# A fused attention and two gated layers: the written order of eight batches, its products and its loads, rearranged

## Chip, cores and metric

One core of a Trainium2 chip. The metric is the device time of one execution in microseconds, lower is better. In the trace PE is TensorE, PEld its weight loads, DVE is VectorE, ACT ScalarE, POOL GpSimd and SP SyncE, which issues the loads and stores.

## What is computed

Batch 8, 8 heads, 576 tokens, head size 64, so 512 columns in all.

```python
kv  = einsum('bhsd,bhde', k, v)          # per head, k^T v
o   = q @ kv;  x = o / rms(o) * g_norm
gate = sigmoid(causal_conv5(x))          # 5 taps on the tokens, per column
x   = (gate * (x @ w_val)) @ w_out
h   = gelu(x @ w_in);  u, v = halves(h)
v_s = w_sg @ layernorm(v) + b_sg         # mixes the 576 tokens
out = x + (u * v_s) @ w_out2
```

## The kernel before

Products are made from fp32r pairs: every operand is split into a high part and a low part, and a 512-column product is 12 matmuls: for each of four 128-row chunks high by high, low weight by high, high by low (`gemm3`). The weights come as 64-bit numbers and are split on the chip too. Tokens go in four tiles of 128 (0 to 3) and a rest of 64 (4); 4 batches share a block of rests (XR), whose own products follow the batches.

The first part (attention, convolution gate, `w_val`, `w_out`, for batches 0 to 7) is written out by hand as a list of steps in `ORDER` and `STEADY`, run one after the other under a manual schedule. Each engine executes its own steps in this order; semaphores hold a step until its inputs are there. Nothing but the list moves a step past another. Behind the list follow batch 7's last products (`val`, then `out`), the rests of batches 4 to 7 and the second layer, which the tile framework's own scheduler places; it can put such later instructions between the last steps of the list.

A step's name is a letter, a batch and a tile or column block:

- `o` product q by kv (PE, 128-column fp32), `q` its squares (ACT), `r` sums (DVE), `m` mean (POOL with a star, else ACT), `w` root (POOL), `s` scale (DVE, with a star ACT), `t` transpose (PE).
- `h`, `x` high part and full copy of the transposed tile (ACT), `l` its low part (DVE). A `t`'s PSUM bank is free when all three have read it. There are eight banks.
- `p`: tap, `pbmj` is batch b, block m, tap j (tap 0 on ACT, 1 to 4 on DVE); `S` sigmoid (ACT). `gX`, `gL`, `gr` (written `g0X`) put the rest columns of x and of the gate into the block XR.
- `v` product with `w_val` (PE), `z` times gate (DVE), `Z`, `u` high and low part (ACT; DVE, with a star POOL), `y` product with `w_out` (PE), `Y` copy (ACT; the last of a batch stores it). `/a-n` is a part of a product. Batch 8 stands for the rests of batches 0 to 3.
- `kv` product k by v (PE), `k` its copies (ACT, some DVE). `a`, `b`, `D`: the steps that split `w_val`, `w_out` and, for pieces a to s, `w_in` and `w_out2`; digits 0 to 4 and `t` are DVE, `a` and `h` ACT, `s` POOL. `c` does the convolution weights. `~3` asks for three filler products.
- `L`: loads on SP's queue: `LK`, `LV`, `Lq`, `La`, `Lb`, `LD`, `Lcw`, `Lg`. K and V have one buffer each. `LM` is no load but a memset on POOL: 64 rows of V's last chunk are zero padding. `W30` is 30 filler products.

`Attention.load_kv` (L342) issues the memset right behind the loads for batches 0 to 2; for later batches the list has `LM3` to `LM7`. `load` (L851) and `act_part` (L896) turn names into instructions. The list ends with taps, sigmoids and weight pieces; its last PE step is `y63`, and `moe.val(0)` (v70, behind the list) comes next on PE.

Of the kernel before, what the change touches and what calls it, by code (L numbers as in the profile page):

```python
# [38 lines left out]
ORDER = """
W30 La0 La1 LK0a LV0a LK0b LV0b LK0c LV0c Lq0a Lq0b Lg La2 La3 Lb0 Lcw a1a a0a a01 a00 a10 kv0a a02 a11 a12 kv0b a13  # L40
a14 a03 k03b k01b a0h k02b k03a k02a k00b k01a k00a a04 o01~3 q01 o03 r01 a20 q03 LK1 o02 a2a r03 a21 q02 o04 a3a m01*
w01 a30 m03* r02 o00 q04 a31 a0l a22 a32 a23 m02* q00 w02 a1h Lq1 a1l s01* a0c w03 a33 r00 ca s02 r04 b0a a2h s03 a24
b01 t01 a3h t02 m00* m04 c0 Lb1 h02 w00 w04 t03~1 c1 a2l s00 h03 h01 a34 x01 b00 t00 c2 s04 x02 kv1 x03 x00 b02 h00
l03 c3 a1c b03 c4 b04 c5 k1b k1a t04 x04 a3l l02 p020 LK2 b1a o11 l01 l00 q11 o12 a3c o14 p021 p000 b10 g0X p022 q12
r11 b0h p023 p001 o13 a2c r12 p002 m12 b11 p024 p030 m11* w11 o10 q14 q13 b12 b0l r13 q10 Lb3 r10 w12 Lb2 p031 v01 b0c
m13* S02 Lq2 p003 b13 p010 m10 w13 s11* w10 v03 s13* p032 s10* p011 t11 kv2 LK3 LM3 v00 p004 p012 p033 b1h v02 S00 k2a
p013 s12* b14 b20 p014 S01 b1s p034 z01 r14 z00 k2b h11 b2a S03 t13 Z01 b1+ Z00 g0L m14* t10 b21 t12 x13 x11 w14 b30
h10 s14 o22 o21~3 u00* l11 g0r z03 h13 Z03 z02 l10 l13 t14 h12 o24 l12 o23 b22 u01* o20 Lq3 LDa LDb q24 x10 q23 b3a
r23 Z02 q22 u03* x14 q20 q21 x12 b31 m23* w23 b23 b32 r22 b24 r21 r20 u02* m20* p110 b33 p120 r24 v11 p111 v12 p121
b2h p112 p122 p100 s23* m24 m21* y01 b2s p101 p123 b2+ p124 w21 p130 y00 s21* Y01 v13 p131 w20 m22* g1X b34 S12 y02  # L50
Y00 p132 w24 t23 b3h b3s s24* w22 t21 p113 p133 s22* b3+ p102 p134 y03 p114 Y02 s20* g1L S11 h23 p103 v10 h21 z11 p104
z12 l21 Z11 t22 S13 Z12 z13 S10 l23 Z13 h22 t24 z10 u11* t20 Z10 l22 u12* u10 h20 u13* x21 Y03 x23 x24 l20 x22 x20 g1r
"""

STEADY = """
kv3a/0-8 kv3a/8-12 kv3b y10 LK4 p220 y11 p210 p221 Daa p222 p230 k3 Da1 p211 p200 y12 p223 p212 Da0 Da2 p201 o30 p213
y13 Da3 q30 p202 p203 p224 r30 o31 p204 m30* v20 w30 p231 S20 q31 Da4 p214 Y12 r31 S21 o32 Dah z20 m31* Y13 Das v21
Z20 w31 p232 p233 s30 u20* o33 Dat LM4 s31 t30 q33 v22 Db0 h30 r33 q32 z21 m33* S22 w33 p234 Dba Y11 r32 g2X o34 Db1
S23 m32* s33 w32 Z21 t31 z22 v23 Y10 u21 g2r x31 g2L LDc Db2 q34 Lq4 Db3 Z22 x30 u22* kv4a/0-8 z23 Dbh h31 kv4a/8-12
s32 Z23 r34 kv4b Db4 m34* Dbs LDd t32 w34 u23 LK5 y20/0-11 h32 Dbt x32 Dca Dc1 Dc0 Dc2 t33 s34 y21/0-5 h33 l32 k4 l33  # L60
y20/11-1 y21/5-7 x33 Dc3 Dc4 Dch l31 LDe Dcs t34 y22 Dct x34 l30 p300 Dda p301 p310 p302 p320 o40 Y21 p303 y23 p330
p311 g3X Y20 Dd0 p312 q40 p304 o41 p321 S30 r40 v30 q41 p331 m40* w40 p322 Dd1 Dd2 p313 o42 r41 v31 q42 s40 m41* w41
Y22 z30 p323 p314 o43 p324 S31 Z30 t40 p332 v32 q43 r42 Y23 p333 S32 m42* u30* s41 r43 o44 z31 w42 z32 Z31 t41 Lq5 v33
p334 q44 m43* Z32 w43 Dd3 s42 Ddh S33 u31 g3r u32* s43 t42 r44 y30/0-9 Dds z33 m44* Dd4 Z33 LM5 Ddt LDf w44 h42 u33
t43 x42 y31/0-9 De0 Dea x40 s44 h41 g3L l42 x41 y30/9-2 x43 De1 y31/9-2 De2 y30/11-1 De3 y31/11-1 Deh t44 De4 y32 Des
LDg x44 Det p430 Df0 l41 p420 p410 y33 Dfa p411 p400 p431 Y32 Y31 p401 p412 v80 Y33 Df1 h40 Df2 p402 v81 p413 p421
kv5a/0-8 l40 kv5a/8-12 p403 kv5b p404 z80 v82 k5 z81 Y30 Df3 v83 Z81 z82 Z80 LK6 u81 Z82 u80* o50 z83 Dfh p414 o51 q50
Dfs h43 r50 y80/0-5 g4X u82* y81/0-5 l43 q51 y82/0-1 Z83 y80/5-1 r51 y81/5-1 y82/1-5 m50* Df4 w50 y83/0-4 Dft LDh
y80/6-2 p422 y81/6-2 Dga y82/6-2 y83/4-1 y80/8-1 Dg0 y81/8-1 m51* y82/8-1 u83 y83/5-2 w51 y80/9-2 y81/9-2 p432 y82/9-2
y83/7-4 Dg1 v40/0-3 Dg2 Dg3 Dgh y80/11-1 s50 y81/11-1 y82/11-1 y83/11-1 Dgs Y81 v40/3-9 S40 Dg4 s51 Y82 LDi Y83 p433  # L70
S41 o52 p423 t50 Dgt q52 t51 p424 Dha v41 Y80 p434 Dh0 Dh1 Dh2 Dh3 Dhh z40 Dhs o53 Z40 LM6 Dh4 v42 z41 LDj q53 r52 S43
Dht Z41 m52* g4L u40* Dia x51 h51 o54 Di1 w52 Di0 Di2 v43 r53 q54 Lq6 Dih Di3 S42 u41 Dis m53* Di4 w53 z42 LDk
kv6a/0-8 Dit Z42 kv6a/8-12 r54 Dja s52 h50 kv6b m54* u42* z43 x50 s53 t52 Z43 LK7 w54 Dj0 g4r Dj1 h52 Dj2 Dj3 Djh u43
y40 x52 LM7 Djs l50 s54 t53 Dj4 y41 x53 l52 LDl h53 Djt Dk0 Dka k6 Dk1 Dk2 Y40 Dk3 t54 l51 Dkh y42 x54 Dks l53 p500
Dk4 Dkt p520 LDm p501 p530 p502 o60 Dla Dl1 p531 y43 q60 p510 p532 p503 p521 o61 Dl0 r60 v50 p522 q61 m60* w60 g5X Dl2
p511 p504 p512 o62 p523 v51 q62 r61 S50 s60 m61* Y43 w61 p533 Y41 p524 o63 r62 t60 p513 q63 m62* v52 Dlh s61 S52 Dl3
Y42 p514 Dls z50 S51 r63 Z50 o64 Dl4 m63* w62 Dlt t61 Lq7 z51 v53 h61 LDn p534 Dma w63 q64 Dm0 g5L Z51 z52 x61 u51 S53
kv7a/0-8 u50* s62 h60 kv7a/8-12 z53 Z52 Dm1 kv7b r64 Z53 u52* l60 t62 s63 m64* y50/0-9 w64 x62 Dm2 u53 h62 Dm3 Dmh k7
Dms s64 t63 y51/0-4 Dm4 h63 Dmt LDo x60 y50/9-2 l63 Dna y51/4-2 Dn0 x63 y50/11-1 Dn1 y51/6-6 Dn2 g5r Dn3 Dnh l61 Dns
t64 l62 y52 x64 Dn4 Dnt LDp p600 p610 p601 Y51 p611 p630 o70 p602 Doa y53 p612 q70 Y50 Do0 p603 p620 Do1 p621 o71 p631  # L80
Do2 v60 q71 p613 Y52 r70 Doh p622 m70* w70 r71 o72 p614 v61 m71* Do3 S61 p604 w71 q72 s70 Y53 p623 S60 p632 o73 p624
t70 r72 q73 v62 S62 z60 m72* w72 h70 p633 Z60 s71 p634 o74 u60* r73 s72 t71 q74 v63 z61 Dos h71 z62 m73* g6r w73 Z61
r74 Z62 Do4 u61 S63 LDq m74* t72 x70 Dot y60/0-8 u62* s73 h72 z63 Dpa g6X w74 Dp1 Z63 l71 t73 Dp0 y61/0-8 u63 h73 Dp2
x73 s74 x71 Dp3 y60/8-1 l73 x72 y61/8-1 y60/9-2 Dph g6L y61/9-2 l72 Dps y60/11-1 y61/11-1 t74 Dp4 y62 Dpt LDr x74 Dq0
l70 p700 p710 p701 Dqa p711 Y61 y63 p730 Dq1 p712 Y62 p702 p720 Dq2 p721 Dqh Y63 Dq3 p722 Dqs Dq4 p713 Dqt p714 Dra
Y60 Dr0 p703 S71 LDs Dr1 p723 Dr2 p704 Drh Dr3 S70 p731 Drs p732 Dr4 p733 Drt p724 Dsa p734 S72 Ds1 S73 Ds0 Ds2
Ds3 Dsh Ds4 Dss Dst
"""
# [1029 lines left out]
```

## Time and profile before

| | us |
|---|---|
| median of 3 runs (716.17 to 716.47) | 716.29 |
| profiled execution | 717.12 |
| its span, first to last instruction | 715.3 |
| PE busy | 706.4 |
| DVE busy | 571.6 |
| ACT busy | 362.2 |
| POOL busy | 161.8 |
| mean DMA rate | 114 GB/s |

The written list takes the first 265 us of the span. An engine's idle time costs nothing unless it makes the engine wait that ends last, so the stretches have to be read one by one: which engine is full in each, and what the next product on PE waits for.

### The profile page before, as it was taken

Reading aid. Unit: us, or ns where it says so; the run is one execution under the profiler, and the core shown is the slowest. Engines: PE = TensorE matmul, PEld = TensorE weight load, DVE = VectorE, ACT = ScalarE, POOL = GpSimd, SP = SyncE. Lnnn points to the kernel's source line nnn. Section 1 sums busy time; section 2 is a strip of 40 time slices with the busy share of each in tenths; the row PEclk is TensorE's granted clock in tenths of the full one; section 3 lists DMA queues with packets and bytes.
Section 4 is the critical chain, followed back from the end, with each engine's and each line's share of the span. In section 5 each row is a group of like instructions: output and inputs, shape, how many; then the busy total and the mean of one; then the engine's idle time right before and its main releaser. Section 6 shows DMA issues by size and latency. Waiting matters only on the chain.

```text
span 715.3 us, 11743 instructions
## 1 busy us (share of the span) xinstructions
PE 706.4 (99%) x4462; PEld 618.3 (86%) x4462; DVE 571.6 (80%) x1111; ACT 362.2 (51%) x747; POOL 161.8 (23%) x180
## 2 busy tenths in 40 slices
...
GB/s 299 309 305 178 16 185 224 115 126 227 190 108 155 75 31 172 146 149 38 97 103 30 75 89 58 53 67 89 76 145 40 65 74 75 59 60 45 103 1 89
DMA packets 57241, 81.20 MB, mean 114 GB/s; under 512 B 3680, under 2 KB 30304, under 8 KB 56160
## 3 DMA queue, kind: packets, MB, share of 16 engines
...
HBM read 61.56 MB, written 18.87 MB: 112 GB/s over the span
## 4 chain that ended last, share of the span: by engine, by line
PE 90%; DMA 5%; DVE 3%; issue 1%; SPq 0%; ACT 0%; ACTq 0%
PE sg L740 17%; PE hv L631 14%; PE out L303 14%; PE y L303 12%; PE hu L303 12%; PE val L303 12%; PE o L400 4%; PE kv L379 2%; PE xT L436 2%; DMA Q<-in_qT_dram 2%; PE hur L303 2%; DMA V<-in_v_dram 1%; DVE G L499 1%; DMA raw<-in_w_in_dram 1%; DMA wiu<-in_w_val_dram 1%
## 5 line engine op out<-in xcount | busy, mean ns | idle before, releaser
L499 DVE SCALAR_TENSOR_TENSOR G<-X,cw,G 128x576 f32<-128x576 f32 x128 | 101.5, 824 | 4.2 <-ACT G L496 3.9
L303 PE MATMUL y<-Z,WOh 128*128 128x512 f32 (+1 forms) x320 | 96.5, 375 | 0.0
L643 POOL TENSOR_TENSOR bmv<-bmv,mhalf 128x1 f32<-128x1 f32 x36 | 20.1, 559 | 333.6 <-DVE bmv L642 333.6
L631 PE MATMUL hv<-wiv,X1h 128*128 128x512 f32 x256 | 83.1, 390 | 0.0
L303 PE MATMUL out<-Z,K 128*128 128x512 f32 x256 | 82.9, 389 | 0.0
L303 PE MATMUL hu<-X1h,wiu 128*128 128x512 f32 x256 | 79.4, 390 | 0.0
L421 POOL TENSOR_TENSOR st<-st,mhalf 128x8 f32<-128x8 f32 x40 | 73.0, 1838 | 2.2
L303 PEld LDWEIGHTS y<-Z,WOh 128*128 128x128 f32 x320 | 57.9, 188 | 9.8
L620 ACT ACTIVATE T<-T 128x512 f32<-128x512 f32 x68 | 43.0, 632 | 44.0 <-DVE T L617 43.8
L303 PE MATMUL y<-Z,WOl 128*128 128x512 f32 (+1 forms) x160 | 58.0, 368 | 0.0
L303 PEld LDWEIGHTS out<-Z,K 128*128 128x128 f32 x256 | 48.1, 188 | 9.9
L631 PEld LDWEIGHTS hv<-wiv,X1h 128*128 128x128 f32 x256 | 47.7, 188 | 9.8 <-ACT X1h L608 0.2
L303 PEld LDWEIGHTS hu<-X1h,wiu 128*128 128x128 f32 x256 | 46.6, 188 | 8.3
L741 DVE SCALAR_TENSOR_TENSOR T<-sg,gln,WOl 128x288 f32<-128x288 f32 x64 | 32.8, 516 | 24.8 <-PE sg L740 24.7
L303 PE MATMUL hu<-X1l,wiu 128*128 128x512 f32 x128 | 50.0, 390 | 0.0
L631 PE MATMUL hv<-wiv,X1l 128*128 128x512 f32 x128 | 49.9, 390 | 0.0
L303 PE MATMUL out<-Z,V 128*128 128x512 f32 x128 | 49.8, 389 | 0.0
L752 ACT ACTIVATE Z<-T 128x512 fp32r<-128x512 f32 x32 | 20.2, 631 | 58.2 <-DVE T L751 58.2
L400 PEld LDWEIGHTS o<-kvbd,Q 128*128 128x128 f32 x320 | 39.9, 191 | 2.6 <-ACT kvbd L391 0.5
L400 PE MATMUL o<-kvbd,Q 128*128 128x128 f32 x320 | 40.7, 275 | 0.3 <-ACT kvbd L391 0.3
L303 PE MATMUL val<-X0h,WV 128*128 128x512 f32 x128 | 40.7, 399 | 0.0
L303 PE MATMUL val<-X1h,WV 128*128 128x512 f32 x128 | 40.0, 396 | 0.1
...
## 6 DMA issues: line engine op xcount, KB each, us to landing
y_main<-Y SPq DMA_DIRECT2D x8, 1024.0 KB, 4.6
...
K<-in_k_dram SPq DMA_DIRECT2D x7, 1024.0 KB, 7.4
V<-in_v_dram SPq DMA_DIRECT2D x7, 1024.0 KB, 9.4
...
```

What stands on the lines that cost most here:

```text
L303: nc.tensor.matmul(ps, lhsT=a[:, kt, msl], rhs=x[:, kt], start=(i == 0), stop=(i == 3 * NK - 1))
L379: nc.tensor.matmul(self.pk[j][h, h], lhsT=self.k[:, t, js][:, h], rhs=self.v[:, t, js][:, h], start=(t == 0), stop=(t == 4))
L400: nc.tensor.matmul(po[:, j * P:(j + 1) * P], lhsT=self.q[:, j, o:o + P], rhs=bd[:, j, :], start=True, stop=True)
L421: nc.gpsimd.tensor_tensor(st[:, 2], st[:, 1], mhalf, op=ALU.pow)
L436: nc.tensor.transpose(pt[:, j * P:(j + 1) * P], i["xo"][:, j * P:(j + 1) * P], ident)
L499: stt(gate[:, m], x32[:, m, j:j + S], cw3[:, m, j:j + 1], gate[:, m], op0=ALU.mult, op1=ALU.add)
L620: act(w, w, AF.Tanh, scale=CG * AG)
L631: nc.tensor.matmul(ps, lhsT=a[:, kt], rhs=p2["wiv"][:, w, kt], start=(i == 0), stop=(i == 3 * NK - 1))
L643: nc.gpsimd.tensor_tensor(mv[:, 3:4], mv[:, 2:3], mhalf[:, 0:1], op=ALU.pow)
L740: nc.tensor.matmul(ps, lhsT=a[:, msl], rhs=w, start=(n == 0), stop=(n == len(mm) - 1))
L741: later(0, lambda: stt(vs[:, sl], ps, gln_s[:, m:m + 1], p2["bsg"][:, sl], op0=ALU.mult, op1=ALU.add))
L752: act(g[:, 0], x, AF.Copy)
```

## The change

`ORDER` and `STEADY` become one list with the same 1168 names in another order, and three new names, `LM0`, `LM1` and `LM2`: the memsets that `load_kv` did for batches 0 to 2 are now steps of their own. Every other step is there once, as before, with the same star and the same fillers. The o products of a batch now mostly stand together, the transposes too, and the tiles of a batch come in other sequences. Among the loads, V's first half leads, and `La1` follows batch 0's K and V. At the list's end `l71` and `l73` stand behind `y63`.

The diff, cut to the two lists' starts and ends and the code:

```diff
 ORDER = """
-W30 La0 La1 LK0a LV0a LK0b LV0b LK0c LV0c Lq0a Lq0b Lg La2 La3 Lb0 Lcw a1a a0a a01 a00 a10 kv0a a02 a11 a12 kv0b a13
-a14 a03 k03b k01b a0h k02b k03a k02a k00b k01a k00a a04 o01~3 q01 o03 r01 a20 q03 LK1 o02 a2a r03 a21 q02 o04 a3a m01*
-w01 a30 m03* r02 o00 q04 a31 a0l a22 a32 a23 m02* q00 w02 a1h Lq1 a1l s01* a0c w03 a33 r00 ca s02 r04 b0a a2h s03 a24
...
-"""
-
-STEADY = """
-kv3a/0-8 kv3a/8-12 kv3b y10 LK4 p220 y11 p210 p221 Daa p222 p230 k3 Da1 p211 p200 y12 p223 p212 Da0 Da2 p201 o30 p213
...
-r74 Z62 Do4 u61 S63 LDq m74* t72 x70 Dot y60/0-8 u62* s73 h72 z63 Dpa g6X w74 Dp1 Z63 l71 t73 Dp0 y61/0-8 u63 h73 Dp2
-x73 s74 x71 Dp3 y60/8-1 l73 x72 y61/8-1 y60/9-2 Dph g6L y61/9-2 l72 Dps y60/11-1 y61/11-1 t74 Dp4 y62 Dpt LDr x74 Dq0
-l70 p700 p710 p701 Dqa p711 Y61 y63 p730 Dq1 p712 Y62 p702 p720 Dq2 p721 Dqh Y63 Dq3 p722 Dqs Dq4 p713 Dqt p714 Dra
-Y60 Dr0 p703 S71 LDs Dr1 p723 Dr2 p704 Drh Dr3 S70 p731 Drs p732 Dr4 p733 Drt p724 Dsa p734 S72 Ds1 S73 Ds0 Ds2
-Ds3 Dsh Ds4 Dss Dst
+LV0a La0 LK0c LV0b Lcw W30 LK0a LV0c LK0b LM0 Lg La1 Lq0a a00 Lq0b La2 La3 Lb0 ca a0a c1 a01 a02 kv0a c0 a03 kv0b k03b
+k00a LK1 a1a k00b c2 k01b k03a k02a k02b k01a o01~3 a11 c3 a10 c4 a04 o00 a12 q01 a0h r01 o02 q00 a13 m01* a1h c5 r00
+w01 a0l q02 a2a o03 r02 m00* a14 o04 m02* q03 w02 a21 s01* r03 a1l Lq1 a20 Lb1 a22 m03* Lb2 w03 q04 s02 b0a r04 t02
+a2h t01 a23 LM1 a3a a30 w00 a24 h01 b01 h02 s03 m04 a1c a31 t03~1 w04 s00 x02 a2l a0c a32 x01 l02 t00 x03 s04 h03 b00
...
+s72 Z61 p634 u61 S63 t73 z62 t72 Dot v63 Z62 s74 x72 u62* s70 Dpa s71 x73 Dp0 g6r Dp1 h72 Dp2 t70 Dp3 Dph t74 Dp4 x70
+t71 Dps z63 LDr x74 y60/0-8 Dpt h70 l72 Dqa Z63 Dq0 Dq1 y61/0-8 x71 Dq2 u63 Dqh p730 Dq3 Dq4 Dqs p710 l70 LDs y60/8-1
+y61/8-1 Y53 y62 p731 p700 Dqt p732 Dra p701 Dr1 y61/9-2 Dr0 p702 y60/9-2 y61/11-1 Dr2 y60/11-1 p703 y63 Drh h71 Dr3
+p704 p720 Drs l71 Y62 Dr4 p711 Drt p721 Dsa Y60 Ds0 Ds1 Y63 p722 h73 Ds2 S70 p712 Dsh Y61 Ds3 p733 Dss l73 p713 p723
+p714 p734 S71 p724 S73 Ds4 S72 Dst
 """
...
@@ -863,7 +860,7 @@
             piece[0]()
             piece[2]()
         elif what in ("K0c", "V0c"):
-            atts[0].load_kv((), (kind == "V",))
+            atts[0].load_kv((), (kind == "V",), clear=False)
         elif kind in "KV" and i[0] == "0":
             atts[0].load_kv(K0[i[1]], (kind == "V",), False)
         elif kind == "M":
@@ -872,7 +869,7 @@
             w_piece(i)[0]()
         elif kind in "KV":
             if kind == "K":
-                atts[int(i)].load_kv(clear=int(i) < 3)
+                atts[int(i)].load_kv(clear=False)
         elif kind == "q":
             atts[int(i[0])].load_q({"a": ((0, 2 * P),), "b": ((2 * P, S),), "": ((0, S),)}[i[1:]])
         elif what == "cw":
@@ -957,11 +954,6 @@
                 busy(int(op[1:]))
             elif op in ("kv0a", "kv0b"):
                 atts[0].kv("ab".index(op[3]), False)
-            else:
-                act_part(op.rstrip("*"), op[-1] == "*")
-        for op in STEADY.split():
-            if op[0] == "L":
-                load(op[1:])
             else:
                 act_part(op.rstrip("*"), op[-1] == "*")
     marks = [latest()] * 4
```

## Rows read from the trace of the kernel before

**Rows 1.** Page: busy time of each engine (share, instructions); DMA issues with median us to landing.
```profile
PE 706.4 (99%) x4462; PEld 618.3 (86%) x4462; DVE 571.6 (80%) x1111; ACT 362.2 (51%) x747; POOL 161.8 (23%) x180
...
V<-in_v_dram SPq DMA_DIRECT2D x7, 1024.0 KB, 9.4
```
**Rows 2.** Table by stretches: stretch, us, engines' busy us (instructions), granted clock, DMA share, GB/s.
```profile
0.00:5.00 5.00, 3.15 (x15) 3.15 (x16) 0.00 (x0) 1.49 (x2) 2.74 (x14) 1.00 0.65 204
5.00:10.00 5.00, 5.00 (x47) 5.00 (x46) 2.61 (x6) 1.86 (x3) 0.00 (x0) 1.00 0.99 345
10.00:15.00 5.00, 3.02 (x83) 2.68 (x81) 1.57 (x4) 0.00 (x0) 0.00 (x0) 1.00 1.08 324
15.00:35.00 20.00, 18.19 (x172) 13.38 (x168) 16.65 (x39) 16.19 (x40) 10.63 (x11) 1.00 1.00 315
35.00:80.00 45.00, 45.00 (x323) 39.07 (x322) 44.43 (x72) 42.90 (x128) 27.48 (x22) 1.00 0.58 197
...
265.00:276.00 11.00, 11.00 (x50) 9.13 (x49) 11.00 (x22) 4.63 (x9) 3.51 (x3) 1.00 0.35 119
...
700.00:716.00 16.00, 12.16 (x77) 10.83 (x76) 4.28 (x8) 0.00 (x0) 0.00 (x0) 0.97 0.29 100
```
**Rows 3.** Waits of PE: who waited for whom, us in total, times, longest.
```profile
PE kv L379 <- DMA V<-in_v_dram: 2.3, 3, 1.8
PE xT L436 <- DVE T L429: 0.8, 2, 0.4
```
**Rows 4.** Timeline of PE, first 35 us: start, us, instruction, [idle before, releaser].
```profile
13.13 1.15 PE L379 MATMUL kv<-V,K 128*64 128x64 f32 x32 [1.78 <-DMA V<-in_v_dram]
...
16.31 5.02 PE L400 MATMUL o<-kvbd,Q 128*128 128x128 f32 x40 [0.28 <-ACT kvbd L391]
...
30.96 2.09 PE L379 MATMUL kv<-V,K 128*64 128x64 f32 x64 [0.36 <-DMA V<-in_v_dram]
```
**Rows 5.** Line 340 (memset of V): duration ns min/median/max, first and last start.
```profile
L340 POOL MEMSET V<- x8: 517/518/523, 2.3 to 194.2; 64x512 f32 x8
```
**Rows 6.** Timeline of DVE, 253 to 264 us.
```profile
253.27 0.42 DVE L278 TENSOR_TENSOR wiu<-cv 128x256 fp32r<-128x256 f32 x1
253.61 0.69 DVE L429 TENSOR_TENSOR T<-o,st 128x512 f32<-128x512 f32 x1
254.21 0.68 DVE L531 TENSOR_TENSOR T<-val,G 128x512 f32<-128x512 f32 x1
...
255.86 0.28 DVE L194 TENSOR_SCALAR cv<-raw 128x256 int32<-128x256 int32 x1
256.06 0.68 DVE L540 TENSOR_TENSOR Z<-T,Z 128x512 fp32r<-128x512 f32 x1
...
257.80 0.74 DVE L452 SCALAR_TENSOR_TENSOR X1l<-xT,gcol,X1h 128x512 fp32r<-128x512 f32 x1
...
258.46 0.90 DVE L482 TENSOR_TENSOR XR<-X,XR 128x256 fp32r<-128x256 f32 x1
...
261.79 1.54 DVE L499 SCALAR_TENSOR_TENSOR G<-X,cw,G 128x576 f32<-128x576 f32 x2
...
263.25 0.42 DVE L482 TENSOR_TENSOR XR<-X,XR 128x256 fp32r<-128x256 f32 x1
```
**Rows 7.** Timeline of PE around the end of the written order.
```profile
249.75 0.71 PE L303 MATMUL val<-X0h,WV 128*128 128x512 f32 x2
...
264.95 1.52 PE L303 MATMUL val<-X1h,WV 128*128 128x512 f32 x6
...
277.64 1.56 PE L303 MATMUL val<-XR,WV 128*128 128x256 f32 x12
279.05 0.63 PE L303 MATMUL y<-Z,WOh 128*128 128x512 f32 x2
```
**Rows 8.** Timeline of ACT at the end of the written order.
```profile
261.57 0.40 ACT L478 ACTIVATE XR<-X 128x256 fp32r<-128x256 f32 x1
```

More of the change, by code (lines that the diff above doesn't have):

```diff
@@ L39 @@
 ORDER = """
-W30 La0 La1 LK0a LV0a LK0b LV0b LK0c LV0c Lq0a Lq0b Lg La2 La3 Lb0 Lcw a1a a0a a01 a00 a10 kv0a a02 a11 a12 kv0b a13
-a14 a03 k03b k01b a0h k02b k03a k02a k00b k01a k00a a04 o01~3 q01 o03 r01 a20 q03 LK1 o02 a2a r03 a21 q02 o04 a3a m01*
-w01 a30 m03* r02 o00 q04 a31 a0l a22 a32 a23 m02* q00 w02 a1h Lq1 a1l s01* a0c w03 a33 r00 ca s02 r04 b0a a2h s03 a24
-b01 t01 a3h t02 m00* m04 c0 Lb1 h02 w00 w04 t03~1 c1 a2l s00 h03 h01 a34 x01 b00 t00 c2 s04 x02 kv1 x03 x00 b02 h00
-l03 c3 a1c b03 c4 b04 c5 k1b k1a t04 x04 a3l l02 p020 LK2 b1a o11 l01 l00 q11 o12 a3c o14 p021 p000 b10 g0X p022 q12
@@ L45 @@
[L45 to L49, printed above, removed]
@@ L50 @@
-b2h p112 p122 p100 s23* m24 m21* y01 b2s p101 p123 b2+ p124 w21 p130 y00 s21* Y01 v13 p131 w20 m22* g1X b34 S12 y02
-Y00 p132 w24 t23 b3h b3s s24* w22 t21 p113 p133 s22* b3+ p102 p134 y03 p114 Y02 s20* g1L S11 h23 p103 v10 h21 z11 p104
-z12 l21 Z11 t22 S13 Z12 z13 S10 l23 Z13 h22 t24 z10 u11* t20 Z10 l22 u12* u10 h20 u13* x21 Y03 x23 x24 l20 x22 x20 g1r
-"""
-STEADY = """
-kv3a/0-8 kv3a/8-12 kv3b y10 LK4 p220 y11 p210 p221 Daa p222 p230 k3 Da1 p211 p200 y12 p223 p212 Da0 Da2 p201 o30 p213
-y13 Da3 q30 p202 p203 p224 r30 o31 p204 m30* v20 w30 p231 S20 q31 Da4 p214 Y12 r31 S21 o32 Dah z20 m31* Y13 Das v21
@@ L58 @@
[L58 to L82, printed above, removed]
@@ new lines @@
+k00a LK1 a1a k00b c2 k01b k03a k02a k02b k01a o01~3 a11 c3 a10 c4 a04 o00 a12 q01 a0h r01 o02 q00 a13 m01* a1h c5 r00
+w01 a0l q02 a2a o03 r02 m00* a14 o04 m02* q03 w02 a21 s01* r03 a1l Lq1 a20 Lb1 a22 m03* Lb2 w03 q04 s02 b0a r04 t02
+a2h t01 a23 LM1 a3a a30 w00 a24 h01 b01 h02 s03 m04 a1c a31 t03~1 w04 s00 x02 a2l a0c a32 x01 l02 t00 x03 s04 h03 b00
+h00 a33 kv1 b02 a3h a34 x00 l01 b03 l03 t04 k1a LK2 b04 k1b a3l x04 p000 o13 p010 LDa p001 o12 Lb3 q13 l00 o10 q12 r13
+p020 o11 r12 m13* a2c LM2 p011 w13 o14 q11 p002 b1a v01 Lq2 q14 p003 p030 r14 a3c r11 g0X q10 p012 m11* v02 s13* w11
@@ new lines @@
+p004 r10 b0h p031 m10 s11* p013 w10 t13 p021 v00 p014 m12 m14* S00 w12 p032 s10* p033 kv2 w14 z00 S01 b11 s12* p034
+p022 h13 b0l LK3 p023 b2a b20 t12 k2a b10 v03 S03 b12 h12 p024 b0c b13 b1h s14 k2b z01 S02 t10 x13 b21 t14 b14 o21~3
+g0r Z01 g0L z02 Z00 l13 h10 t11 u00* o20 x14 l12 x12 l10 u01* o22 h11 z03 q21 o23 b1s q20 q22 o24 l11 g1X Da0 v10 b1+
+q24 Lq3 b30 Z02 LDb b22 x11 u02* r21 b3a r24 Z03 b23 LM3 x10 u03* y01 r22 q23 p130 r23 m21* p120 p131 m23* m22* p100
+w21 v13 b31 r20 p110 p101 Y01 w23 m24 b24 b2h b32 s21* y00 p111 w22 b2s s23* b2+ m20* p112 w24 y02 s22* p102 b33 w20
@@ new lines @@
+p121 p113 t22 b34 Y02 v12 p122 b3h Daa p103 s20* b3s p123 s24* t21 p132 v11 b3+ h21 p114 Y00 p104 g1L y03 S10 p124 S11
+p133 S12 z10 z11 t24 p134 Z10 kv3a/0-8 Y03 Da1 Da2 kv3a/8-12 Z11 z12 S13 u11* kv3b x24 z13 Z12 u10 g2X t20 LM4 LK4 k3
+u12* t23 Z13 h22 u13* y11 x21 l22 h23 g1r h20 o31 x22 l20 o32 x23 l21 x20 o30 l23 p200 o34 p220 p201 o33 q30 p221 q34
+y10 p202 p230 Lq4 Y11 Da3 p222 q33 p210 p203 p231 y13 Y10 g2L q32 Da4 q31 r33 Dah p211 m33* Das r31 kv4a/0-8 r30 m31*
+kv4a/8-12 w33 r32 kv4b p232 p223 w31 y12 LK5 Dat p224 m30* s33 S22 w30 p204 Dba LDc k4 s31 v20 S20 m32* Db0 w32 p212
@@ new lines @@
+Y13 s30 p233 p213 t30 t31 Db1 z20 t33 h31 o43 s32 Z20 p234 v22 h30 l31 r34 Db2 m34* Db3 LM5 Dbh p214 q43 v21 Y12 Dbs
+z22 S23 l30 w34 h33 Db4 x30 l33 LDd Z22 t32 Dbt x31 r43 o41 u22* Dca s34 S21 o40 u20* h32 z21 o44 q40 q41 Dc1 t34 Dc0
+Z21 r40 v23 q44 r41 m40* x34 w40 l32 g2r x33 x32 y21/0-5 p310 z23 Dc2 o42 Dc3 Dch u21 p320 Dcs r44 Z23 y20/0-11 m43*
+p321 m44* w44 Dc4 p311 LDe s40 w43 Dct u23 y23 Dda q42 p300 m41* r42 g3X Dd1 y21/5-7 m42* s43 p330 w42 p312 p313 y22
+w41 p301 p302 p322 y20/11-1 Y22 v32 s42 Y21 g3L p323 p303 p331 v31 p332 p324 p333 p314 t43 v30 p304 S31 Y20 s41 S30
```

19 lines of the change are left out of this document (added).

## Prediction, made before the change was run

> **What bounds the kernel now.** I read the engines' busy shares first: TensorE (PE) is busy 706.4 of 715.3 us, VectorE (DVE) 571.6 [rows 1]. So a new order with the same work can win only what PE now loses, 8.9 us, and can lose as much as it makes PE wait. The table by stretches says where the 8.9 us lie: 1.85 in the first five microseconds, 1.98 between 10 and 15, 1.81 between 15 and 35, and 3.1 behind 700, where 12.16 of the last 15.3 us are busy; that leaves 0.1 for all the rest, and none for the stretches 35 to 80 and 265 to 276 [rows 2]. In two stretches another engine is full as well: DVE is busy 44.43 of 45 between 35 and 80, and 11.00 of 11 between 265 and 276, where the written order ends and the tile scheduler's part begins [rows 2]. There a badly placed DVE step becomes a wait of PE. The list of PE's waits names what can be won: 2.3 us for the loads of V, 0.8 for the normalised tiles that the transposes read [rows 3].
>
> **The change, its start.** The same steps are issued; I counted every name in both lists, and only the three memset steps are new names, for memsets that the loads did until now. PE does the same products with the same three plus one plus three filler products, so PE's work is equal and only waits can differ. On SP's queue the first loads now come as V0, weight piece a0, K0's and V0's remainders and second halves, with a1 behind all of batch 0's K and V. K0 and V0 are complete after about 3.0 MB instead of 3.5 MB; at the 300 GB/s that the first stretches move [rows 2] the last piece lands some 1.7 us sooner, but then the larger half of the product (48 instructions instead of the last 16) is still to do. The second part now starts at 13.13, after 1.78 us of waiting [rows 4]; I put the end of this product 0.5 us earlier. The first o product started at 16.31 [rows 4]; it needs Q, which is now behind a1, K0, V0 and the small loads: the same bytes, and no gain. What follows is the same on PE up to batch 1's kv product, in another order, and that product ran until its load landed: its last 64 instructions start at 30.96, after 0.36 us of waiting for V [rows 4], with the DMA engines full (share 1.00) between 15 and 35 [rows 2]. The loads ahead of it (four a pieces, b0, K0, V0, Q0, conv weights) are the same set in the new list. So whatever the start gains is lost again at this load: 0, at best 0.5, at worst 1 if POOL's chain for the first tiles runs later. The memsets of V's padding move on POOL's queue, batch 1's now between two roots; one lasts 0.518 us [rows 5], and the root behind it, then a scale and a transpose, come 0.5 us later, still some 1.5 us ahead of 30.96: nothing.
>
> **The middle, 35 to 250 us.** PE loses 0.1 us there, so nothing but its changes between kinds of product can be won. To see whether something is to be lost I added, by such start-to-start times as [rows 6] gives, the DVE work that the list puts ahead of each PE step, and compared it with the PE work ahead of the same step. In the old list the tightest step has 5.8 us of PE work more than DVE work before it (the filler ahead of the third o product of batch 2), and as DVE was full there [rows 2] while PE did not wait, that margin was just enough. In the new list the tightest such step behind 30 us has 7.2, so DVE should hurt less. The same sum for ACT gives 6.0 in both lists. From 100 us on the chain from an o product to its transpose has 15 to 28 us of PE work in the new list, but for one tile, against 10 in the old. K's and V's loads have 14 us or more from a free buffer to their use, against 9.4 from the issue of V to its landing [rows 1]. I take 0, with 0.8 gained and 1.0 lost as bounds.
>
> **The end of the written order, where I see the cost.** The products of batch 7 that follow the list (v70 to v73) read the split x of all four 128-token tiles, so the third matmul of v70 needs the steps l70 to l73. In the old list all four stand ahead of y63, the last PE step. In the new list l71 and l73 stand behind it, l73 on DVE behind most of the taps of batch 7 and the weight splits p, q, r and s. DVE cannot begin z62 before v62 has ended. From z62 to l73 the new list holds on DVE: 6 multiplies, scales or subtractions of 128x512, 4 l steps, 11 taps, 12 short and 11 long weight steps. The start-to-start times in the same stretch are 0.60 (a scale or u step), 0.66 (l), 0.73 (half of the two taps), 0.20 (short weight step) and 0.34 (long) [rows 6]: 3.6 + 2.64 + 8.03 + 2.4 + 3.74 = 20.4 us. That sum is low: from z63 at 254.21 to 263.25 the same way of adding gives 8.05 us for 17 instructions that took 9.04, a factor of 1.12, part of it steps such as the subtraction of 0.90 us at 258.46 [rows 6]. So l73 ends 20.5 to 22.9 us after v63 starts; I take 21.7. PE has v63, three transposes and y60 to y63 in that time; the same set took from 249.75 to 264.95, 15.2 us [rows 7], and v70's first two matmuls 0.45. The wait is 21.7 - 15.65 = 6.0 us (4.9 to 7.3; at least 3.6 when the sum begins at z63 alone, which cannot start before v63 ends).
>
> What can fill it: the tile scheduler puts later products where PE would wait. It did so at 277.64, where a group of 12 products of the rest tokens (val from XR) stands inside the y products and takes 1.41 us [rows 7]; four such groups exist. They need batch 7's rest columns, whose copy on ACT and subtraction on DVE came at 261.57 and 263.25, both before y63 ended and well ahead of the list's end [rows 6, 8]. In the new list the transpose that they follow (t74) is issued some 11 us before y63 ends, so the rest columns may be ready. Banks limit it: when y63 ends, y61 and y63 and the transposed tile that l73 reads hold three of eight and v70 one more, so I count on three groups, 4.2 us. 6.0 - 4.2 leaves 1.8 us. Afterwards DVE has less left than before (l73 is followed by 4.5 us of list, against 15 behind y63 in the old one), so no later wait is added and the fillers are not missed.
>
> **Sum.** Start 0, middle 0, end +1.8. The profiled execution took 717.12 us, with a span of 715.3, and stands 0.8 above the median of 716.29; the change is carried over as it is: 718.9 for a profiled execution, 718.1 for the median.
>
> **Rivals.** (A) Not slower: the filler covers the whole wait. Its place is the gap behind y63, its price the 5.6 us of all four groups. It decides if the rest columns are ready when y63 ends, four banks are free, and l73 lies less than 5.6 us behind; then 716.3 + 0.4, less up to 0.8 from the middle: 715.5 to 717. For it: the scheduler left no wait of PE between 265 and 276 with DVE full [rows 2]. Against it: the banks, and a sum that already runs to 7.3 us. (B) No filler, because DVE, full in this stretch, gets the rest subtraction only after l73: 716.3 + 6.0 = 722.3 (720.5 to 723.6). For it: the rest products need both halves, and the new list leaves DVE no gap from z63 on. Against it: at 263.25 the subtraction stands among the list's own steps, though DVE was full [rows 6]. (C) As B, and TensorE runs slower after the wait. The first 15 products took 3.15 us, 0.21 each, the next 47 took 5.00, 0.106 each [rows 2], so PE starts at half speed, though the granted clock is given as 1.00 there; that start lasted some 2.8 us and cost half of it. One more such start would make 722.3 + 1.4 = 723.7. The waits inside this trace, up to 1.8 us, show no such fall, and 6 us occur nowhere, so the rows speak neither for nor against. The Trainium skill ("TensorE: Matmul & The Clock Gate", Part 1: The HAM clock gate) has an idle engine go back from 2.4 to 1.2 GHz; no row here shows that. (D) Faster: the start is not held by batch 1's load and keeps 0.5 to 1 us, the middle gives its 0.8, and the end is filled as in A: 714.6. Against it: the 0.36 us wait and the full DMA engines.
>
> **How the numbers follow.** A measurement of this kernel can tell about 0.2%, 1.4 us, from no change. Forecast (partly filled, 0.8 to 4 us left, 717.1 to 720.3): 0.42; A: 0.30; B: 0.16; C: 0.04; D: 0.08. Faster by over 0.2% is D, 0.08. Within 0.2% are A and the lowest fourth of the forecast, 0.40. Slower is the rest, 0.52. As both signs hold weight: the forecast's own range is 717.1 to 720.3; the range that leaves out no more than D's lower part, C and B's upper end is 715.2 to 722.4.
>
> **What would show it.** The new trace should show PE without waits from 35 us to the first val product on X1 of batch 7; there the third matmul should wait for a DVE instruction that writes X1l, with val products from XR ahead of it or among it. If the XR products still stand only inside the y products and PE is idle for 4 us or more, B is right; if PE has no idle time there, A. Twice the start-to-start time in the products behind an idle stretch would be C. Batch 1's kv product should still end near 33 us; earlier than 32.3 would make D possible, and an end later than 34 would mean that my chain for the first tiles is wrong. What would make the prediction wrong altogether is a wait in the middle, above all of a transpose or a y product between 50 and 100 us, where DVE and ACT have less than a microsecond to spare.

## The result, and the profile after

The changed kernel takes 728.17 us (median of 4 runs, 726.64 to 728.47), the kernel before 716.38 in the same comparison: 11.8 less. The ratio of the means is 1.0145, with an interval of 1.0101 to 1.0188 (one run of before, at 721.05, weighs in its mean). So the change makes it about 1.5% slower; the forecast was 718.1, with a range that ended at 722.4. The profiled execution of the changed kernel took 728.31 us with a span of 726.5, 11.2 more than the 715.3 of before. Its code has three lines fewer, so line 300 is 303 of before, and so on. One execution of b_pool2, the last run below, took 757.55 us at a granted clock of 0.88 and is not counted.

Page of the changed kernel: busy time, and the chain that ended last.

```profile
PE 709.5 (98%) x4462; PEld 620.6 (85%) x4462; DVE 570.4 (79%) x1111; ACT 360.8 (50%) x747; POOL 165.1 (23%) x180
...
PE 70%; DVE 11%; POOL 8%; ACT 4%; issue 4%; DMA 2%; SPq 0%; POOLq 0%; DVEq 0%; ACTq 0%
```

Against [rows 1] VectorE has no more work than before, but PE is busy 3.1 us longer with the same 4462 instructions, and POOL, which is busy for 23%, now holds 8% of the chain. The table by stretches (columns as in [rows 2]) says where the time went:

```profile
0.00:35.00 35.00, 28.70 (x309) 25.01 (x310) 20.82 (x48) 19.76 (x45) 13.54 (x24) 1.00 0.98 320
35.00:265.00 230.00, 226.78 (x1659) 195.17 (x1659) 214.18 (x379) 160.62 (x361) 120.77 (x109) 1.00 0.43 145
...
265.00:276.00 11.00, 6.64 (x24) 5.12 (x23) 11.00 (x23) 5.54 (x12) 2.30 (x2) 0.84 0.38 144
276.00:290.00 14.00, 14.00 (x56) 11.39 (x55) 9.37 (x15) 5.77 (x10) 2.58 (x2) 0.88 0.46 160
...
290.00:500.00 210.00, 210.00 (x1182) 186.43 (x1181) 158.93 (x335) 89.56 (x173) 16.14 (x25) 1.00 0.24 79
```

In the first 35 us PE is busy 28.70 us against 29.36 (the sum of the four rows of before in [rows 2]). Between 35 and 265 it loses 3.2 us, where before it lost 0.1. Between 265 and 276 it loses 4.4, where before it was full, and the granted clock, 1.00 in all stretches of before up to 276, falls to 0.84 and 0.88. From 290 to 700 nothing is lost. PE's timeline shows the fall, and in the last line where the products that I had counted on as filler went:

```profile
268.59 0.39 PE L300 MATMUL y<-Z,WOh 128*128 128x512 f32 x1
273.34 3.78 PE L300 MATMUL val<-X1h,WV 128*128 128x512 f32 x8 [4.36 <-ACT X1h L441]
276.92 0.63 PE L300 MATMUL val<-X1l,WV 128*128 128x512 f32 x1
277.34 1.05 PE L300 MATMUL val<-X1h,WV 128*128 128x512 f32 x2
...
279.42 0.39 PE L300 MATMUL val<-X1l,WV 128*128 128x512 f32 x1
279.65 0.63 PE L300 MATMUL val<-X1h,WV 128*128 128x512 f32 x2
...
298.04 1.56 PE L300 MATMUL val<-XR,WV 128*128 128x256 f32 x12
```

PE waits 4.36 us for h73 (ACT, X1h). Then the 15 products from 273.34 to 279.65 take 6.31 us; at the 0.23 that one takes from 279.42 on they would take 3.4. One stands alone for 0.42 (276.92 to 277.34): that is the 1.2 GHz level instead of 2.4, after an idle stretch, and it costs 2.9 us. Wait and clock together are 7.2; with 3.1 more lost in the middle and 0.7 at the start that is 11.0 of the 11.2. Rows of ACT and VectorE in the same place:

```profile
271.30 0.44 ACT L181 ACTIVATE cv<-raw 128x256 f32<-128x256 f32 x1 [1.57 <-DVE V L275]
271.64 1.06 ACT L552 ACTIVATE Y<-y 128x512 f32<-128x512 f32 x2
272.60 0.69 ACT L441 ACTIVATE X1h<-xT,gcol 128x512 fp32r<-128x512 f32 x1
...
275.05 0.74 DVE L449 SCALAR_TENSOR_TENSOR X1l<-xT,gcol,X1h 128x512 fp32r<-128x512 f32 x1
```

h73, the row at 272.60, stood in ACT's queue behind the evictions Y60 and Y63 and behind Dsa, which waited 1.57 us until VectorE had used the buffer of the previous weight piece. l73 ended another 2.5 us later; the high products of v70 to v73 covered it.

### The profile page after: what moved, and what is told of

Same layout as the page of the kernel before. It is cut to its first block, busy times and chain, and to the rows that moved or that the text cites. A ratio compares the mean times of both kernels' runs of the same rounds, so it can differ in the third digit from the quotient of the medians.

```text
span 726.5 us, 11741 instructions
## 1 busy us (share of the span) xinstructions
PE 709.5 (98%) x4462; PEld 620.6 (85%) x4462; DVE 570.4 (79%) x1111; ACT 360.8 (50%) x747; POOL 165.1 (23%) x180
## 4 chain that ended last, share of the span: by engine, by line
PE 70%; DVE 11%; POOL 8%; ACT 4%; issue 4%; DMA 2%; SPq 0%; POOLq 0%; DVEq 0%; ACTq 0%
PE sg L737 16%; PE out L300 14%; PE hv L628 14%; PE hu L300 12%; POOL st L418 6%; PE val L300 6%; PE y L300 4%; DVE G L496 3%; DVE st L407 2%; PE hur L300 2%; POOL st L414 1%; DMA Q<-in_qT_dram 1%; PE o L397 1%; POOL cv L277 1%; DVE T L528 1%
## 5 line engine op out<-in xcount | busy, mean ns | idle before, releaser
L496 DVE SCALAR_TENSOR_TENSOR G<-X,cw,G 128x576 f32<-128x576 f32 x128 | 99.6, 810 | 1.9 <-ACT G L493 1.6
L300 PE MATMUL y<-Z,WOh 128*128 128x512 f32 (+1 forms) x320 | 94.5, 371 | 0.2 <-POOL Z L537 0.2
L738 DVE SCALAR_TENSOR_TENSOR T<-sg,gln,WOl 128x288 f32<-128x288 f32 x64 | 32.7, 515 | 24.6 <-PE sg L737 24.5
L300 PE MATMUL val<-X1h,WV 128*128 128x512 f32 x128 | 42.5, 419 | 5.4 <-ACT X1h L441 4.4
L397 PEld LDWEIGHTS o<-kvbd,Q 128*128 128x128 f32 x320 | 38.3, 192 | 3.6 <-DVE kvbd L390 1.0
```

What stands on the lines that cost most here:

```text
L300: nc.tensor.matmul(ps, lhsT=a[:, kt, msl], rhs=x[:, kt], start=(i == 0), stop=(i == 3 * NK - 1))
L397: nc.tensor.matmul(po[:, j * P:(j + 1) * P], lhsT=self.q[:, j, o:o + P], rhs=bd[:, j, :], start=True, stop=True)
L496: stt(gate[:, m], x32[:, m, j:j + S], cw3[:, m, j:j + 1], gate[:, m], op0=ALU.mult, op1=ALU.add)
L738: later(0, lambda: stt(vs[:, sl], ps, gln_s[:, m:m + 1], p2["bsg"][:, sl], op0=ALU.mult, op1=ALU.add))
```

## Experiments

Theory: the loss has two places. At the end, h73 and l73 stand too far back, and the wait slows TensorE. In the middle, the o products of a batch now come in a bunch, so that five roots (w steps, 1.64 to 2.4 us each) run one after another on POOL, and the one needed first may be last; POOL and ACT in the changed kernel, and the val product of PE that ends the row:

```profile
67.77 5.67 POOL L418 TENSOR_TENSOR st<-st,mhalf 128x8 f32<-128x8 f32 x3
73.52 0.27 POOL L414 TENSOR_SCALAR st<-st 128x8 f32<-128x8 f32 x1
73.87 4.15 POOL L418 TENSOR_TENSOR st<-st,mhalf 128x8 f32<-128x8 f32 x2
78.05 2.77 ACT L424 ACTIVATE T<-o,st 128x64 f32<-128x64 f32 x13 [1.46 <-POOL st L418]
79.85 0.72 PE L300 MATMUL val<-X1h,WV 128*128 128x512 f32 x2 [1.05 <-ACT T L424]
```

w20 is the last of these five, ACT's scale s20 waits for it, and v11 for the bank that s20 frees. Rivals: the loss is that of the start; or VectorE is simply short of time along the list; or there is no slower clock, only the wait.

**The end alone, taken out of the changed list (a_tail).**

```diff
-h70 l72 Dqa ... y63 Drh h71 Dr3 p704 p720 Drs l71 ... p722 h73 Ds2 ... Dss l73 p713
+h70 h71 h73 l72 l71 l73 Dqa ... y63 Drh Dr3 p704 p720 Drs ... p722 Ds2 ... Dss p713
```

> The changed kernel with only its end undone: h71, h73, l71 and l73 stand again ahead of y63 (behind h70 and l72). Theory 1 (the end of the list costs 4.4 us of waiting for h73 and l73 and about 2.9 us of products at half pace behind it): 728.2 - 7.2 = 721.0, the granted clock stays at 1.00 between 260 and 295 us, and the first val product of batch 7 follows y63 without a wait. Rival (DVE has the same work in any order, so the wait only moves from v70 to the y products that need the gate of batch 7): 726 or more, with PE idle behind 275 us. About 721 also means that some 4.5 us of the loss lie ahead of the end.

It took 720.94 us (720.39 to 721.54; before 716.65; ratio 1.0057, 1.0042 to 1.0072). Between 265 and 276 PE is full at a granted clock of 1.00. So the end is worth 728.17 - 720.94 = 7.2 us and the rest of the list 4.3.

```profile
265.00:276.00 11.00, 11.00 (x50) 9.14 (x49) 11.00 (x23) 5.88 (x12) 1.69 (x2) 1.00 0.41 151
```

**The end alone, put into the list of before (b_late).**

```diff
-(before's places of h73 and l73, ahead of y63)
+... y63 ... Y60 h73 ... p704 l73 ...
```

> The kernel before with only the end done: h73 behind Y60 and l73 behind p704, both behind y63; all else as before (the memsets stand where the loads did them). From y63's start its list holds 9.0 us of DVE work up to p704, and l73. Theory 1: v70 waits about 4 to 6 us and the products behind the wait run slow: 716.3 + 6.5 = 722.8 (720 to 725). Rival (the late steps hurt only together with the rest of the new list, which brings PE to the end later or earlier against DVE): within 1 us of 716.3.

It took 723.37 us (722.33 to 724.72; ratio 1.009, 1.0073 to 1.0107): 6.7 more than before from two steps, with a like wait (4.91 us, again for h73) and the same slow products behind it.

```profile
269.24 3.78 PE L300 MATMUL val<-X1h,WV 128*128 128x512 f32 x8 [4.91 <-ACT X1h L441]
...
265.00:276.00 11.00, 6.76 (x20) 5.42 (x21) 10.96 (x20) 3.58 (x8) 2.62 (x2) 0.69 0.35 121
```

**The same wait, with TensorE kept at work (a_fill).** 20 filler products (two instructions each, results unused) ahead of v70, in the changed list.

```diff
     marks = [latest()] * 4
+    idle[0] = 20
```

> The changed kernel with 20 filler products (4.5 us) between y63 and v70, in the time in which PE waited; they write v70's own bank and depend on nothing. Theory 1a (the slow products behind the wait are a cost of their own, because TensorE falls from 2.4 to 1.2 GHz in it): the wait stays hidden behind the fillers, the products behind them run at 0.227 us each, granted clock 1.00, and the time is 728.2 - 2.3 = 725.9 (725.3 to 726.5). Rival (products behind the wait are slow for another reason, such as operands that arrive late): no change, 728.2, with 0.45 us per product as before.

It took 725.6 us (725.38 to 725.87): 2.6 less than the changed kernel, though the work grew. The filler fills the wait, the granted clock stays at 1.00, and the eight products that took 3.78 take 2.11.

```profile
268.36 4.62 PE L321 MATMUL val<-ident 128*128 128x128 f32 x40
272.89 2.11 PE L300 MATMUL val<-X1h,WV 128*128 128x512 f32 x8
275.39 0.50 PE L300 MATMUL val<-X1l,WV 128*128 128x512 f32 x1 [0.39 <-DVE X1l L449]
...
265.00:276.00 11.00, 10.62 (x67) 9.15 (x66) 11.00 (x23) 5.45 (x11) 2.30 (x2) 1.00 0.36 140
```

So the slow clock behind an idle TensorE is shown: 2.9 us in the trace, 2.6 in the times. The faster products then wait 0.39 us for l73, which about makes up the difference.

**The start alone (a_start).**

```diff
+(the changed list up to t04, then the steps that are left, in before's order)
```

> The changed list up to and with t04 (about 33 us), then the remaining steps in before's order. Theory (the start is worth 0: the product of batch 1 ends 0.3 us earlier with the new order, and the rest is before's): 716.3, 715.8 to 717.0. Rival (the new order of the loads delays something later, or the steps that the new start postpones crowd the next stretch, where VectorE is full): 717.5 or more, with waits of TensorE between 35 and 80 us that before doesn't have.

716.99 us (715.96 to 719.05, 11 runs) against 716.53 (15 runs): ratio 1.0006, 0.9997 to 1.0015. The start costs 0.5 us, with bounds of -0.2 and 1.1.

**Roots made cheap in the changed list (a_tail_root).** The list is that of a_tail.

```diff
-nc.gpsimd.tensor_tensor(st[:, 2], st[:, 1], mhalf, op=ALU.pow)
+nc.gpsimd.tensor_scalar(st[:, 2], st[:, 1], 1.0, 0.0, op0=ALU.mult, op1=ALU.add)
```

> The kernel of the undone end in which, besides, the root on POOL is left out: the step that takes the power -0.5 (1.7 to 2.3 us each) is a multiplication by 1 on POOL (about 0.2 us) instead, so the normalisation of x leaves its root out and the output is not the reference's. Theory 2 (the waits of PE between 75 and 260 us come from five roots in a row on POOL, because the new list puts a batch's o products together): these waits of t30, o64, t60, t61, t70 and v11 go, and the time is 721.0 - 4 = 717.0 (716 to 718). Rival (they come from DVE, which is full and gets to the scales late): 720.5 to 721.0, the same waits for DVE's scale.

719.29 us (718.36 to 721.05), 1.65 less than a_tail and between the two expectations. The waits ahead of v11, t30, t60 and t70 are gone; one of 0.85 us ahead of o64 is new (for k6, on ACT).

**The control: roots made cheap in the list of before (b_root).** The edit is the same.

> The list of before, with each reciprocal root on POOL (line L418) replaced by a multiplication by 1 (so the normalised tiles are not the reference's; only the time is read). It is the control for the run that did the same to the changed list. Theory (the five roots in a row on POOL cost TensorE time only where the new list bunches them): before's TensorE waits for no root, so the time stays at 716.6, within 0.7 (715.9 to 717.3). Rival (cheaper roots shorten any list): it falls by as much as in the changed list, 1.6 us, to 715.0 or less.

718.95 us (718.48 to 719.97; ratio 1.0037, 1.0024 to 1.0049): slower by 2.4, which neither side had. With less work on POOL, VectorE is busy 575.5 us instead of 571.6, and transposes of batches 5 and 6 wait for it: 0.34, 0.70 and 0.91 us. A tap that took 0.81 (first line, from the trace of before) takes 1.57 beside a product on POOL that the short roots brought forward (then POOL, VectorE and the transposes of PE, all with short roots):

```profile
220.24 0.81 DVE L499 SCALAR_TENSOR_TENSOR G<-X,cw,G 128x576 f32<-128x576 f32 x1
...
220.34 1.30 POOL L537 TENSOR_TENSOR Z<-T,Z 128x512 fp32r<-128x512 f32 x1
...
220.69 1.57 DVE L496 SCALAR_TENSOR_TENSOR G<-X,cw,G 128x576 f32<-128x576 f32 x1
...
224.65 0.66 PE L433 MATMUL xT<-ident,T 128*128 128x128 f32 x4 [0.34 <-DVE T L426]
228.08 0.66 PE L433 MATMUL xT<-ident,T 128*128 128x128 f32 x4 [0.70 <-DVE T L426]
257.67 0.55 PE L433 MATMUL xT<-ident,T 128*128 128x128 f32 x3 [0.91 <-DVE T L426]
```

That this tap and others like it make the transposes late is argued from the order of the rows. So shortening the roots does not isolate their queue: it also moves POOL's products. The 1.65 us above can't be put down to the queue alone, and the roots were left as they are in the reorderings that follow.

**POOL's kind of work (b_prod).** In the list of before, a product of two large tiles and a short multiplication in place of each root.

```diff
-nc.gpsimd.tensor_tensor(st[:, 2], st[:, 1], mhalf, op=ALU.pow)
+nc.gpsimd.tensor_tensor(junk[:, 0], junk[:, 1], junk[:, 1], op=ALU.mult)
+nc.gpsimd.tensor_scalar(st[:, 2], st[:, 1], 1.0, 0.0, op0=ALU.mult, op1=ALU.add)
```

> The list of before; each reciprocal root on POOL is replaced by a product of two 128x512 f32 tiles in SBUF that nobody reads, and a multiplication by 1 (so the normalised tiles are not the reference's). POOL is then busy about as long as with the root (1.3 + 0.2 against 1.64 us), but with a product of large tiles. Theory (VectorE's instructions whose operands all lie in SBUF are held while POOL works on a large product, and not while it works on a root; this made the kernel before slower when its roots were shortened, as the products on POOL then came at another time): VectorE's busy time rises from 571.6 us by 15 to 30 (40 products, each holding 0.4 to 0.7 us), and the time by 5 to 20, to 722 to 737. Rival (POOL's kind of work doesn't matter to VectorE): 716 to 717.5, and VectorE's busy time within 4 us of before's.

739.59 us (737.37 to 739.78; ratio 1.0318), 2.6 above the theory's upper end and far from the rival. VectorE is busy 598.0 us, 26.4 more than before and 22.5 more than with short roots alone (b_root), though POOL, at 160.2, works no longer than before:

```profile
PE 710.9 (97%) x4462; PEld 619.6 (84%) x4462; DVE 598.0 (81%) x1111; ACT 362.8 (49%) x747; POOL 160.2 (22%) x221
...
L499 DVE SCALAR_TENSOR_TENSOR G<-X,cw,G 128x576 f32<-128x576 f32 x128 | 112.1, 906 | 3.9 <-ACT G L496 3.7
```

**The queue itself (a_pool).** From a_tail, only POOL's order is changed (and s64 on VectorE), so that the root needed first runs first.

```diff
-w24 y02 s22* p102 b33 w20          | r30 m31* kv4a/8-12 w33 .. w31 .. m30* .. w30
+y02 s22* p102 b33 w20 w24          | r30 m31* kv4a/8-12 w33 m30* w30 .. w31
-m64* w64 .. w60 .. w61 .. s64 s61  | m70* Doh m74* .. w71 .. w70
+w60 .. w61 m64* w64 .. s61 s64     | m70* w70 Doh m74* .. w71
```

> The changed list with h71, h73, l71 and l73 moved ahead as in the run without the wait at the end (720.9), and with eight steps moved on POOL's queue in three batches, so that the root which TensorE needs first runs first: w24 behind w20; m30 and w30 behind w33; m64 and w64 behind w61, and s64 behind s61 on VectorE; w70 behind m70. Nothing is cheaper, only the order is other. Theory (TensorE waits in the middle because a root queues behind roots that are needed later): w20 ends 2.1 us earlier and the wait of 1.07 ahead of v11 goes, w30 2.3 us earlier (0.19 goes), w60 and w61 1.6 us earlier (0.69 and 0.38 go): together 2.3 us, so 718.6 (718.0 to 719.4). Rival (VectorE's and ACT's own order sets these waits, the roots are only inputs that come in time): under 0.7 us gained, 720.2 or more.

720.8 us (719.59 to 721.52): no gain on a_tail, so the time is what the rival had said. But the trace says something else. The waits ahead of v11, t60 and t61 are gone; in their place t30 waits 1.72, because on VectorE s31, which needs the later root w31, still stood ahead of s30 (PE's row, then VectorE's):

```profile
109.88 1.50 PE L433 MATMUL xT<-ident,T 128*128 128x128 f32 x12 [1.72 <-DVE T L426]
...
107.51 0.69 DVE L426 TENSOR_TENSOR T<-o,st 128x512 f32<-128x512 f32 x1 [1.81 <-POOL st L418]
```

I had reordered one queue and not the one that reads from it.

**Bank steps earlier (a_pool_k6).**

```diff
-Y80 Z41 Dj4 h51 Djs LDl k6
+k6 Y80 Z41 Dj4 h51 Djs LDl
```

> As the kernel with the steps moved on POOL's queue, and besides k6 (the copies that free the banks of batch 6's kv product, on ACT) moved six steps ahead, before Y80. Theory: the wait of 0.5 to 0.85 us ahead of o64 (TensorE waits for a bank that k6 frees; k6 runs at 194.13 though its product ended at 191.45) goes, so 0.5 to 0.8 us less than the kernel without this move: 717.9. Rival (ACT is full there, and what k6 passes, x54, h51 and Y80, is then late in its place): no gain, or a new wait ahead of the next kv or y product, 718.6 or more.

720.85 us (719.99 to 721.13): no gain. It tells nothing: in the profile of the kernel that it is compared with, o64 does not wait at all.

**Both queues in order (a_pool2).** From a_pool.

```diff
-w30 .. k4 s31 .. Db0 w32 p212 Y13 s30   | m74* p611 g6X w71 .. p612 p604 w74 .. u60*
+w30 .. k4 s30 s31 .. Db0 w32 p212 Y13   | p611 g6X w71 .. p612 p604 .. u60* m74* w74
```

> The run with the roots reordered on POOL (720.8), with two further moves, again without changing any work. That run lost its gain ahead of t30: w30 ran first, but on VectorE the scale s31, which waits for the later root w31, still stood ahead of s30, so VectorE waited 1.81 us and t30 1.72; here s30 goes ahead of s31. And ahead of t70 VectorE waited 1.87 us for the product u60 on POOL, which stood behind the root w74 that is needed only later; here m74 and w74 go behind u60. Theory (what costs in the middle is each in-order queue with a step that waits for a late root ahead of a step that doesn't): the waits ahead of t30 (1.72, and the 0.19 of the first form) and t70 (0.73) go, 2.5 us together: 718.3 (717.5 to 719.2). Rival (VectorE's sum of work is short in these stretches, so a cured wait comes back at the next transpose): 719.8 or more, with waits at t31, t32, t71 or the y products of batch 6.

720.18 us (718.32 to 720.47; before 716.17): again a time that the rival had said. The waits ahead of t30 and t70 are gone, and those that the rival named (t31, t32, t71) did not come; others did. PE's waits between 35 and 265 us:

```profile
PE kv L376 <- DMA V<-in_v_dram: 1.1, 2, 0.8
PE val L300 <- DVE T L528: 1.0, 1, 1.0
PE o L397 <- DMA Q<-in_qT_dram: 0.2, 1, 0.2
```

The first two are again a step in a queue behind one that waits: on VectorE T of batch 2 behind s31, and on SP's queue the loads of batch 7's K and V behind the weight piece LDl, which waited until 195.13 for its buffer.

**All three queues in order (a_pool3).** From a_pool2.

```diff
-k4 s30 s31 v20 S20 m32* Db0 w32 p212   | LDl k6 LK7
+k4 s30 v20 S20 m32* Db0 w32 p212 s31   | LK7 LDl k6
```

> As the run above with s30 and w74 moved (720.2), with two more moves for the two waits of TensorE that appeared there: s31, for which VectorE waited 0.91 us (for the root w31) with the product T of batch 2 queued behind it, goes four VectorE steps later; and the loads of batch 7's K and V go ahead of the weight piece LDl on SP's queue, which waited until 195.13 for its buffer though TensorE had left K's at about 192. Theory (each wait in the middle is a step that stands in an in-order queue behind one that waits longer, SP's queue among them): 1.03 us ahead of v22 and 0.79 + 0.27 us in batch 7's kv product go, and nothing else takes their place: 718.3 (717.5 to 719.1). Rival (the slack of this list is short all along, so the next late step shows at once): 719.5 or more, with TensorE's waits between 80 and 265 us again above 1.5 us.

718.61 us (718.0 to 720.1; before 716.61; ratio 1.0036, 1.0022 to 1.005). In the middle PE is busy 229.55 of 230 us, where a_tail had 227.14, and only one wait is left of the list there (a_tail's row first, then a_pool3's wait and row):

```profile
35.00:265.00 230.00, 227.14 (x1663) 195.86 (x1662) 214.59 (x378) 161.25 (x362) 120.87 (x109) 1.00 0.42 144
...
PE y L300 <- POOL Z L537: 0.2, 1, 0.2
...
35.00:265.00 230.00, 229.55 (x1675) 197.86 (x1674) 217.61 (x385) 162.43 (x364) 121.22 (x109) 1.00 0.43 148
```

The work and the products on TensorE are those of the changed list; 2.4 us of PE's time came back in the trace, 2.3 in the times, and no run of a_pool3 is as slow as the fastest of a_tail (718.0 to 720.1 against 720.39 to 721.54). So the middle's loss was not a lack of VectorE's time but steps that stand in an in-order queue behind one that waits longer.

**Before's start with that rest (b_pool2).** Before's list up to t04, then the rest of a_pool2.

> Before's list up to and with t04, then the changed list with the tail, the roots and the scales moved as in the run above. Theory: the new start costs about 0.4 us in the median (717.0 against 716.5 in the run with the new start alone), so this takes 0.4 less than the run above, 717.9, and with the middle's waits gone all but 1 us of the loss is accounted for. Rival (the new start postpones work of batch 0 and 1, which shows only with the new rest): over 1 us less than the run above, 717.3 or less.

718.87 us (718.47 to 720.86 in four runs; ratio 1.0041, 1.0028 to 1.0055). That is 1.3 less than a_pool2, as the rival had it, but above the time that either side gave (717.9, and 717.3 or less), and the runs of the two kernels overlap. It decides nothing.

What stays open is some 1.5 us of the 2.0 by which a_pool3 is slower than before. In its profile they lie in the first 35 us, where PE is busy 27.70 us against 29.36, with waits of 1.8 us for Q and 1.2 for K. But in a_pool, with the same first steps, that stretch has 30.15, and in a_tail 28.29, so one profile doesn't settle it, and the start alone cost 0.5 (bounds -0.2 and 1.1). None of the kernels beats the one before.

## Why the prediction was wrong, point by point

**The start, forecast at 0 (-0.5 to +1), was right in size, not in its reason.** Batch 1's product ends at 32.7 us, before at 33.05, and the start alone costs 0.5. But in this trace it is not held by batch 1's load. The waits for V [rows 4] are gone; instead an o product waits 0.81 us for Q, where I had put neither gain nor loss, and the transposes t02 and t03 wait 1.06 and 1.43 us for VectorE:

```profile
18.47 1.16 PE L397 MATMUL o<-kvbd,Q 128*128 128x128 f32 x8 [0.81 <-DMA Q<-in_qT_dram]
...
25.12 1.06 PE L433 MATMUL xT<-ident,T 128*128 128x128 f32 x8 [1.06 <-DVE T L426]
...
27.84 0.66 PE L433 MATMUL xT<-ident,T 128*128 128x128 f32 x4 [1.43 <-DVE T L426]
...
30.18 2.55 PE L376 MATMUL kv<-V,K 128*64 128x64 f32 x80
```

**The middle, forecast at 0 (-0.8 to +1), was the first wrong step: it cost 3.1 us.** I summed each engine's work ahead of a PE step and compared sums. Such a sum knows nothing of an engine that stands still with work queued behind the wait. By that sum the tightest step had 7.2 us to spare, and PE lost 3 us in seven waits, none longer than 1.1. I made it for VectorE and ACT and not for POOL at all. I counted the 15 to 28 us from an o product to its transpose as slack, but only from 100 us on; in batch 2, ahead of that, the five roots alone take POOL from 67.77 to 78.02. Behind 100 us the slack did not hold either: four transposes waited there, for up to 0.56 us. The experiments put a number on it: with the same work, reordering three queues gave 2.3 us back. The prediction had said that a wait in the middle would make it wrong altogether, but no rival gave one a price, so the range had no room for it.

**The end, forecast at +1.8, cost 7.2, and three terms failed: the wait, the filler and the clock.** The sum to l73 held, at its upper end: 20.5 to 22.9 us after v63 starts were forecast, and it ended 22.8 after (v63 starts at 252.98, l73 ends at 275.79). But PE came to the end of the list 0.8 us later than I had it, by waits such as the 0.56 us ahead of t70, and the first thing missing was not l73 but h73: I followed the two l steps on VectorE and did not follow h71 and h73 through ACT's queue, where Dsa, Y60 and Y63 stand ahead. So the wait was 4.36, not 6.0.

```profile
252.98 0.71 PE L300 MATMUL val<-X0h,WV 128*128 128x512 f32 x2
...
256.52 1.53 PE L433 MATMUL xT<-ident,T 128*128 128x128 f32 x12 [0.56 <-DVE T L426]
```

The filler, on which 4.2 us rested, did not come: the rest products ran at 298, although their inputs were written by 261. I had inferred from one place [rows 7] that the scheduler puts them into gaps; here it put the high products of v70 to v73 first, which hide l73 but not h73. With h73 and l73 late the rest products even went further back: they begin at 298.04 here and at 293.42 in b_late, but at 277.64 before and at 280.83 in a_tail. Why the scheduler chose so, no run shows. And the slow clock, which I priced at 1.4 us in rival C, cost 2.9: I took it for a loss of half of 2.8 us, by the start of the trace [rows 2], and here it lasted 6.1.

So at the end rival C (no filler, TensorE slower) was what happened; its 7.4 us meet the 7.2, though by a wait that was shorter and a clock that cost more. It had a chance of 0.04, because no row of before had an idle stretch of that length. Here the rule of the Trainium skill ("TensorE: Matmul & The Clock Gate", Part 1: The HAM clock gate) that I had set beside it, that an idle engine goes back from 2.4 to 1.2 GHz, is borne out by the 0.42 us of a product behind the wait against 0.23 later.

**That nothing more is lost after the wait was right:** PE is full from 276 to 700, apart from its slower clock at the start of that stretch.

**Two bounds do not follow from their terms.** B's lower end would be 716.3 + 4.9 = 721.2 and not 720.5, and A's 716.7 - 0.8 = 715.9 and not 715.5. Neither changes the range that was missed.
